# Re-dealing the filter rows of a Fourier layer in SBUF, and copying them by DMA, ahead of a long gated MLP

## The chip, the cores and the metric

The kernel runs on one core of a Trainium2 chip. A core has five engines that run side by side, each with its own queue of instructions: TensorE (PE, matrix products; its weight loads are shown as PEld), VectorE (DVE), ScalarE (ACT), GpSimd (POOL) and SyncE (SP), which here only issues transfers. Transfers run on 16 DMA engines that all queues share. Engines wait for each other through semaphores. SBUF, the on-chip memory, has 128 partitions; PSUM, into which TensorE writes, has eight banks.

The metric is the device time of one execution in microseconds. The kernel before took 485.1 us (median of three runs, 485.1 to 485.33).

## The reference

The input x has 2048 rows (positions) of 576 values. A layer normalisation is followed by a two-dimensional real Fourier transform, a product with a complex filter of 2048 x 289 values (w_r and w_i), and the inverse transform. The result is added to x. A second normalisation is followed by a gated MLP with 4608 hidden units, again added.

```python
h = x + _A_ref(_layernorm(x, axis=-1), A_w_r, A_w_i)
h2 = h + _B_ref(_layernorm(h, axis=-1), B_w_gate, B_w_up, B_w_down)
# _A_ref:  X = rfft2(x);  X = X * (w_r + 1j * w_i);  y = irfft2(X, s=(S, D))
# _B_ref:  (gelu(x @ w_gate) * (x @ w_up)) @ w_down
```

## The kernel before, in words

All transforms are matrix products with tables. The work falls into a start of some 55 us (normalisation, Fourier layer, first part of the second normalisation) and a long MLP part, which is almost pure TensorE work.

The start has these steps, in stages whose order on all engines is written out by hand in strings of codes (`SEQ1`, `SEQF`, `SEQ`). The first transform along positions (line 551) leaves its result in `U`. Then sixteen groups of frequencies, numbered by `GORD` as 1 to 15 and then 0, go through `SEQF`. For group number i: `D`/`d` is the transform along the 576 values (line 640), evicted to `CUS` (three buffers); `B` is a small transform over 16 (line 660), evicted to `YS` (five buffers); `T` (line 673, VectorE) multiplies `YS` by the filter in `WS`, in two instructions, one to `TP` and one to `TR`; `V`/`v` (line 681) and `R`/`r` (line 698) begin the inverse transform, evicted to `V` and `RB`. `RB` goes on to `VR` by small transfers. Evictions are casts at line 606 on ScalarE or VectorE, by the lists `DENG`, `BENG` and `VENG`. Four pairs of PSUM banks are shared by D, B, V and R. The order of the T products is 2, 0, 1, 3, 5, 4, 6, 7, 8 and so on. Then `SEQ` runs the rest of the inverse transform (lines 835 and 852), the addition to x (line 858), the second normalisation and the turn of its result, and the MLP begins (line 944).

The filter tile `WS` has 128 partitions x 2 sides x 2 planes (real 0, imaginary 1) x 16 groups x 289 values. Side jp (0 or 1) is loaded only into one half of the partitions: 64 jp to 64 jp + 63. The product needs each side in both halves, so that half is copied to the other half of the partitions by `dup_w`, in four steps: k = 0 for groups 1 to 5, k = 1 for 6 to 8, k = 2 for 9 to 12, k = 3 for 13 to 15 and 0.

The loads of the filter come in pieces, issued in order. A first half (`hf` 0) has groups 0 to 8, a second half groups 9 to 15. For each plane of each half there are two "up" pieces (`w_up`, one for each side: 32 rows, each contiguous in HBM over its groups) and four "down" pieces (`w_down`, `sl` 0 to 3, two for each side: 16 partitions x 8 or 7 separate rows of 578 bytes, the groups in reverse). `w_zero` fills group 0 of the down rows. In a half of 64 partitions the up pieces fill the lower 32 partitions and the down pieces the upper 32, every second one each. Plane 1 comes before plane 0. All are issued by SP behind the loads of x and the first tables, except the last two down pieces of plane 0 of the second half, which GpSimd issues.

The copies of step 0 are made by engines: GpSimd copies plane 1 and VectorE plane 0, each for both sides. Those of steps 1 to 3 are transfers within SBUF issued by GpSimd, which wait on the semaphores of the pieces. On GpSimd's queue the order is: the normalisation's work, the two down pieces, its two copies, the transfers of step 1, small operations (`NM`), the transfers of steps 2 and 3, the VR transfers. SP waits for the last of the copies before it loads the tables for the rest of the inverse transform (`tab_load`).

`Prog` keeps, for every name that is read or written, who wrote it last. An instruction waits for those it depends on. A key such as `("Wd", 0, jp, pl, 1)` stands for one copied part; the list `dup` says which copied parts the products of each step wait for.

The two lines that decide what a product waits for, and how a copy by an engine looks:

```python
r=[("Y", sl), *dup[(i >= 5) + (i >= 8) + (i >= 12)]] + (wkeys[0] if 1 <= g < 9 else ...)
P.op(DVE, lambda v: v.tensor_copy(dst, src), r=r, w=[(*n, g0)])
```

Of the kernel before, what the change touches and what calls it, by code (L numbers as in the profile page):

```python
# [7 lines left out]
ALU = mybir.AluOpType  # L8

S, D, K2 = 2048, 576, 289  # L10
# [5 lines left out]
NT = 16  # L16
# [30 lines left out]
def build_tables():  # L47
# [52 lines left out]
    for st in range(2):  # L100
        g = 1 - st
        for p in range(128):
            half, r, jj = p // 64, (p % 64) // 4, p % 4
            low = (g + 16 * jj) if half == 0 else _minus_rows(g)[jj]
            k = 128 * r + low
            w = np.exp(-2j * np.pi * ((k * nn) % 2048) / 2048.0)
            if low in (0, 64):
                sl, ri = 0, (0 if low == 0 else 1)
# [8 lines left out]
            if half == 0:  # L117
                sl = jj
                e = np.exp(-2j * np.pi * ((r * nn) % 16) / 16.0)
                ca, cb = e, 1j * e  # L120
            else:
                sl = (128 - low - g) // 16
# [17 lines left out]
    for st in range(2):  # L140
        for jp in range(2):
            for q in range(64):
                half, r, sl = q // 32, (q % 32) // 2, 2 * jp + q % 2
                jj = sl if half == 0 else (4 - sl) % 4 if st else 3 - sl
                po, cut = 64 * half + 4 * r + jj, slice(2 * jp, 2 * jp + 2)
                for m in range(2):
                    for ri in range(2):
                        BN[jp, :, :, st, m, ri, q] = B[st, m + ri, :, cut, :, po].reshape(16, 4)
                for ri in range(2):
                    VN[st, jp, ri, q, 0] = V[st, ri, po, :, :, cut].reshape(2, 16, 4)  # L150
                    VN[st, jp, ri, q, 1] = (1 - 2 * ri) * V[st, 1 - ri, po, :, :, cut].reshape(2, 16, 4)
# [7 lines left out]
    a = np.full((K2 - 1, 1), 2.0)  # L159
# [172 lines left out]
def _build(nc, A_x, A_w_r, A_w_i, B_w_gate, B_w_up, B_w_down, out):  # L332
    P = Prog(nc)
    T = build_tables()
    dram = {n: nc.inline_tensor(_np_bf16(T[n]), name="c_" + n.lower()) for n in T}
    PE, DVE, ACT, SP, POOL = "pe", "dve", "act", "sp", "pool"
# [12 lines left out]
    WS = sb.alloc("WS", [128, 2, 2, NG, K2], BF16)  # L349
# [54 lines left out]
    ATS = sb.alloc("ATS", [128, NT, 128], BF16)  # L404
# [41 lines left out]
    P.dma(SP, FT[:, :, :].rearrange("p a b -> p (a b)"), dram["FTAB"][:, :], "ft", w=["FT"])  # L446
    P.dma(SP, BT[:, :, :, :].rearrange("p a b c -> p (a b c)"), dram["BTAB"][:, :], "bt", w=["BT", "BT1"])

    def w_up(pl, hf):
        g0, g1 = ((0, 9), (9, 16))[hf]  # L450
        src = (A_w_r, A_w_i)[pl].tensor
        for jp in range(2):
            P.dma(SP, WS[64 * jp:64 * jp + 32, jp, pl, g0:g1, :].rearrange("p g k -> p (g k)"),
                  bass.AP(src, (32 * jp + g0) * K2, [[128 * K2, 16], [16 * K2, 2], [1, (g1 - g0) * K2]]), f"w{pl}{hf}", w=[("W", hf, pl, jp)])

    def w_down(pl, hf, sls=(0, 1, 2, 3), eng=SP, sem=""):
        g0, g1 = ((1, 9), (9, 16))[hf]
        src = (A_w_r, A_w_i)[pl].tensor
        for sl in sls:
            p0 = 64 * (sl // 2) + 32  # L460
            P.dma(eng, WS[p0 + sl % 2:p0 + 32:2, sl // 2, pl, g0:g1, :], bass.AP(src, (64 + 16 * (3 - sl) + 16 - g0) * K2, [[128 * K2, 16], [-K2, g1 - g0], [1, K2]]),
                  f"w{pl}{hf}{sem}", w=[("W", hf, pl, 2 + sl)])

    def w_zero(pl):
        for jp in range(2):
            P.dma(SP, WS[64 * jp + 32:64 * jp + 64, jp, pl, 0, :], bass.AP((A_w_r, A_w_i)[pl].tensor, (64 + 32 * jp) * K2, [[128 * K2, 16], [(-16 if jp else 48) * K2, 2], [1, K2]]),
                  f"wz{pl}", w=[("W", 2, pl, jp)])

    for pl in (1, 0):
        w_up(pl, 0)  # L470
        w_down(pl, 0)
    P.dma(SP, VT[:, 0:2, :, :].rearrange("p a b c -> p (a b c)"), dram["VTAB"][:, 0:512], "vt", w=["VT", "VT1"])
    for pl in (1, 0):
        w_up(pl, 1)
        w_down(pl, 1, (0, 1, 2, 3) if pl else (0, 1))
    for pl in (1, 0):
        w_zero(pl)
    GORD = list(range(1, NG)) + [0]
    wkeys = [[("W", hf, pl, h) for pl in range(2) for h in range(6 if hf < 2 else 2)] for hf in range(3)]
# [101 lines left out]
    for w in SEQ1:  # L581
        a = w[1:]
# [9 lines left out]
    for t, w in enumerate(SEQF):  # L592
        k, i = w[0], w[1:].rstrip("abc")
        if k in "DBVR":
            b = min((b for b in used if b not in busy), key=lambda b: used[b])
# [4 lines left out]
        elif k in "dvr":  # L600
            b = FB[k.upper(), int(i)]
# [16 lines left out]
                op = mm(h, o, seqs[h][j], not second and j == 0, second and j == len(seqs[0]) - 1, [prev[o]] if second and j == 0 else [])  # L618
                turn_over.setdefault(key, [None, None])[o] = op

    dup = [[("Wd", 0, jp, pl, 1) for jp in range(2) for pl in range(2)]] + [[("Wd", k, jp, 0, g) for jp in range(2) for g in ((6,), (9,), (13, 0))[k - 1]] for k in range(1, 4)]

    wdv = B_w_down[:, :].rearrange("(c p) d -> p c d", p=128)

# [91 lines left out]
                src = PS[32 * j:32 * j + 32, b0 * 512:(b0 + 2) * 512].rearrange("p (a c) -> p a c", a=2)[:, :, 128 * (i == LAST) + 64 * t_:128 * (i == LAST) + 64 * t_ + 64]  # L716
                ev((ACT, DVE, DVE, ACT)[j], dst, src, keys, [("V", g, 2 + t_)])

    def dup_w(k, jp, pl=slice(0, 2), eng=None):
        a, b = 64 * jp, 64 - 64 * jp  # L720
        n = ("Wd", k, jp, pl.start)
        for g0, g1 in (((1, 6),), ((6, 9),), ((9, 13),), ((13, 16), (0, 1)))[k]:
            dst, src = (WS[q:q + 64, jp, pl, g0:g1, :].rearrange("p a g k -> p a (g k)")[:, :, 1:] for q in (b, a))
            r = [x for x in (wkeys[1] if g0 > 8 else wkeys[0] if g0 else wkeys[0] + wkeys[2]) if pl.start <= x[2] < pl.stop]
            if eng is None:
                op = P.dma(POOL, dst, src, f"wd{k}{jp}", r=r, w=[(*n, g0)])
            elif eng == DVE:
                P.op(DVE, lambda v: v.tensor_copy(dst, src), r=r, w=[(*n, g0)])
            else:
                P.op(POOL, lambda v: v.tensor_scalar(dst, src, 1.0, 1.0, op0=ALU.mult, op1=ALU.mult), r=r + [("ATS", NT - 1)], w=[(*n, g0)])  # L730
        return op if eng is None else None

    w_down(0, 1, (2, 3), POOL, "p")
    for jp in range(2):
        dup_w(0, jp, slice(1, 2), POOL)
        dup_w(0, jp, slice(0, 1), DVE)
    for jp in range(2):
        dup_w(1, jp)
    c = 0
    while c < NT:  # L740
        c1 = c + 1
        while c not in ACT_TILES and c1 < NT and c1 not in ACT_TILES:
            c1 += 1
        src, f, keys = (SA[:, 0, c:c1], -1.0 / D, "SA0") if c in ACT_TILES else (MV1[:, c:c1, 0], -1.0, "MV1")
        P.op(POOL, lambda g, c=c, c1=c1, src=src, f=f: g.tensor_scalar(NM[:, c:c1], src, f, 1.0, op0=ALU.mult, op1=ALU.mult),
             r=[(keys, k) for k in range(c, c1)], w=[("NM", k) for k in range(c, c1)])
        c = c1
    for k in (2, 3):
        for jp in range(2):
            last = dup_w(k, jp)  # L750
    def hold(eng=SP):
        P.op(eng, None, after=[P.ops[PE][-1]])

# [55 lines left out]
    SLOT, last, held, ing = {}, [sorted(used.values()).index(used[2 * b]) - 4 for b in range(4)], set(), False  # L809
    for t, w in enumerate(SEQ):  # L810
        k, i = w[0], int(w[1:].rstrip("ADSP"))
        if k in "INu":
            b = min((b for b in range(2 * ing, 4) if b not in held), key=lambda b: last[b])
# [3 lines left out]
        elif k in "ioUEae":  # L817
            b = SLOT[{"i": "I", "o": "N", "U": "u", "E": "I", "a": "N", "e": "u"}[k], i] // 2
# [145 lines left out]
    for w in SEQ:  # L964
        a = w[1:]
# [53 lines left out]
    for j, c in enumerate(range(NPRE, NT)):  # L1019
        f = DEF0 + DSTEP * j  # L1020
# [77 lines left out]
def bass_sequential_preLN__spectral_gfnet__geglu_ffn__prompt_kernel(  # L1098
    nc, A_x, A_w_r, A_w_i, B_x, B_w_gate, B_w_up, B_w_down, out
):  # L1100
    _build(nc, A_x, A_w_r, A_w_i, B_w_gate, B_w_up, B_w_down, out)
# [28 lines left out]
```

## Time and profile before

| what | us |
|---|---|
| median of three runs | 485.1 |
| the profiled execution's own time | 486.04 |
| its span, from the first to the last instruction | 484.2 |
| TensorE busy | 477.1 |
| VectorE busy | 182.8 |
| ScalarE busy | 145.4 |
| GpSimd busy | 53.2 |

The profile is of one execution. A line of a timeline has the start, the length, the engine, the line of the kernel, the operation and its tiles, and in brackets how long the engine was idle before and what ended it. A "q" behind an engine's name is its queue issuing a transfer. `WS<-in_A_w_r_dram` is a load of the real plane of the filter, `WS<-in_A_w_i_dram` of the imaginary one, `WS<-WS` a copy between the halves. A wait for several semaphores is put down to the one that came last by the profile; where the engine named had long been done, it was another, often a transfer. TensorE's granted clock was 1.000 throughout.

### The profile page before, as it was taken

The page shows a single profiled execution, that of the slowest core. Times are in us where ns is not written, and L with a number is a line of the kernel's source. Part 1 is how long each engine was busy: PE and PEld are TensorE (multiplying, and loading weights), DVE is VectorE, ACT ScalarE, POOL GpSimd, SP SyncE. Part 2 cuts the span into 40 slices and gives each one's busy share as a digit, 9 for nine tenths or more (in the row PEclk, how much of TensorE's full clock was granted, in tenths as well). Part 3 has the DMA queues.
Part 4 walks back from the last instruction along what each step waited for, and adds up shares of the span by engine and source line. Part 5 has one row for each costly group of instructions (what it writes and reads, how often), then busy time and mean ns, then how long its engine had stood idle before and what let it go on. Part 6 is the DMA issues. An engine that isn't in the chain of part 4 may idle for free.

```text
span 484.2 us, 12888 instructions
## 1 busy us (share of the span) xinstructions
PE 477.1 (99%) x5874; PEld 279.1 (58%) x5874; DVE 182.8 (38%) x365; ACT 145.4 (30%) x291; POOL 53.2 (11%) x88
## 2 busy tenths in 40 slices
PE   7999999999999999999999999999999999999998
PEld 4877765544577644444677544444777444444774
DVE  7988755665500144333200234333101233333011
ACT  6998753434300032233200133223100133223000
POOL 7862317010120000000000000000000000000000
PEclk9999999999999999999999999999999999999999
DMA  8955789931430001000000011000000000000000
GB/s 289 217 134 161 249 283 346 333 87 24 161 111 27 26 15 23 20 1 0 3 14 15 26 24 22 14 0 2 3 14 26 14 1 0 1 1 1 3 26 26
DMA packets 28438, 33.19 MB, mean 69 GB/s; under 512 B 12624, under 2 KB 21472, under 8 KB 28384
## 3 DMA queue, kind: packets, MB, share of 16 engines
q1 hardware_dynamic: 24720, 19.87, 14.5%
q0 software_dynamic: 3664, 12.50, 8.0%
q8 instruction: 46, 0.75, 0.7%
q14 instruction: 8, 0.07, 0.1%
HBM read 26.21 MB, written 2.36 MB: 59 GB/s over the span
## 4 chain that ended last, share of the span: by engine, by line
PE 91%; SPq 3%; DMA 2%; DVE 2%; ACT 1%; issue 0%; DVEq 0%
PE PS L944 58%; PE PS L1044 27%; SPq L242 3%; PE PS L1056 2%; DMA WS<-in_A_w_r_dram 1%; PE PS L640 1%; DMA VR<-RB 1%; PE PS L994 1%; DVE XO L858 1%; PE PS L681 1%; ACT YS L606 1%; PE PS L835 0%; PE PS L660 0%; PE PS L1011 0%; PE PS L852 0%
## 5 line engine op out<-in xcount | busy, mean ns | idle before, releaser
L944 PE MATMUL PS<-HT,WG 64*128 64x512 bf16 (+1 forms) x2142 | 233.3, 372 | 0.1
L944 PEld LDWEIGHTS PS<-HT,WG 64*128 64x128 bf16 x2142 | 105.8, 94 | 114.5 <-DVE AT L953 0.2
L952 ACT ACTIVATE GL<-PS 128x512 bf16<-128x512 f32 x144 | 85.7, 596 | 281.7 <-PE PS L944 281.7
L953 DVE TENSOR_TENSOR AT<-GL,PS 128x512 bf16<-128x512 bf16 x144 | 98.8, 687 | 166.0 <-ACT GL L952 166.0
L1044 PE MATMUL PS<-WD,AT 64*128 64x288 bf16 x2160 | 132.9, 283 | 0.0
L1044 PEld LDWEIGHTS PS<-WD,AT 64*128 64x128 bf16 x2160 | 102.5, 94 | 30.6
L1031 DVE TENSOR_TENSOR OS<-PS,XO 128x288 bf16<-128x288 f32 (+2 forms) x32 | 13.3, 453 | 125.5 <-PE PS L1044 118.0
L944 PE MATMUL PS<-HT,WGX 64*128 64x512 bf16 x486 | 53.4, 376 | 0.0
L944 PEld LDWEIGHTS PS<-HT,WGX 64*128 64x128 bf16 x486 | 23.0, 94 | 29.4
L861 ACT ACTIVATE OS<-XO,NM 128x576 bf16<-128x576 bf16 x15 | 11.6, 774 | 11.4 <-DVE XO L1015 11.4
L640 PE MATMUL PS<-FT,U 64*128 64x288 bf16 x160 | 13.7, 284 | 0.3 <-DVE V L606 0.2
L673 DVE TENSOR_TENSOR TP<-YS,WS 128x1024 bf16<-128x1024 bf16 x16 | 11.0, 688 | 1.0 <-PE PS L698 1.0
L494 DVE BATCH_NORM_STATS2 ST<-XO 128x6 f32<-128x288 bf16 x26 | 10.1, 442 | 1.9 <-DMA XO<-in_A_x_dram 1.8
L681 PE MATMUL PS<-VT,TP 64*128 64x128 bf16 x256 | 10.0, 217 | 0.0
L242 POOL DMA_DIRECT2D WG<-in_B_w_gate_dram x9 | 6.1, 679 | 32.2 <-DMA WG<-in_B_w_gate_dram 28.9
L562 ACT ACTIVATE U<-PS 128x384 bf16<-128x384 f32 (+2 forms) x27 | 9.4, 479 | 0.7 <-PE PS L551 0.7
L242 POOL DMA_DIRECT2D WD<-in_B_w_down_dram x9 | 6.7, 755 | 26.1 <-PE PS L1011 26.1
L551 PE MATMUL PS<-ATS,XO 128*128 128x128 bf16 x96 | 8.3, 219 | 1.4 <-POOL ATS L520 1.4
L606 ACT ACTIVATE CUS<-PS 128x576 bf16<-128x576 f32 x14 | 9.0, 654 | 0.7 <-PE PS L640 0.5
L606 ACT ACTIVATE YS<-PS 128x576 bf16<-128x576 f32 x14 | 8.9, 653 | 0.6 <-PE PS L660 0.4
L1056 PE MATMUL PS<-WD,AT 128*128 128x448 bf16 (+1 forms) x72 | 9.0, 286 | 0.0
L681 PEld LDWEIGHTS PS<-VT,TP 64*128 64x128 bf16 x256 | 8.0, 94 | 1.3
(89 smaller groups left out, 230.0 us busy)
## 6 DMA issues: line engine op xcount, KB each, us to landing
WD<-in_B_w_down_dram POOLq DMA_DIRECT2D x9, 576.0 KB, 10.7
WG<-in_B_w_up_dram SPq DMA_DIRECT2D x6, 576.0 KB, 6.4
WG<-in_B_w_gate_dram POOLq DMA_DIRECT2D x6, 576.0 KB, 5.7
out_dram<-OS SPq DMA_DIRECT2D x30, 72.0 KB, 1.7
XO<-in_A_x_dram SPq DMA_DIRECT2D x6, 288.0 KB, 4.5
WGX<-in_B_w_up_dram SPq DMA_DIRECT2D x2, 576.0 KB, 4.7
WGX<-in_B_w_gate_dram POOLq DMA_DIRECT2D x2, 576.0 KB, 5.8
HT<-HN SPq DMA_TRANSPOSE x60, 2.4
```

Source lines behind the costliest of these rows:

```text
L242: fn = lambda e: e.dma_start(out_ap, in_ap)
L606: fn = (lambda v: v.tensor_copy(dst, src)) if eng == DVE else (lambda a: a.activation(dst, src, ACTF.Copy))
L640: return P.op(PE, lambda t: t.matmul(bank(b0 + o, 0, 128, 0, 2 * HK), U[64 * h:64 * h + 64, us, 2 * i:2 * i + 2, :, :], FT[64 * h:64 * h + ...
L673: P.op(DVE, lambda v, dst=dst, y4=y4, w4=w4: v.tensor_tensor(dst, y4, w4, op=ALU.mult), r=[("Y", sl), *dup[(i >= 5) + (i >= 8) + (i >= 12) ...
L681: return P.op(PE, lambda t: t.matmul(bank(b0 + o, 0, 128, 128 * c, 128 * c + 128), TP[64 * h:64 * h + 64, z, o, t_, c:256:2], VT[64 * h:64 ...
L861: P.op(ACT, lambda a, c=c, out=out: a.activation(out, XO[:, c, 0:D], ACTF.Square, bias=NM[:, c:c + 1], accum_out=SB2[:, 1, c:c + 1]), r=[( ...
L944: op = P.op(PE, lambda t, h0=h0, kt=kt, wt=wt, b=b, s=(not second and j == 0), e=(second and j == n - 1): t.matmul(bank(b, 0, 128, c0, c1) ...
L952: P.op(ACT, lambda a: a.activation(GL[:, s2, :], bank(b0), ACTF.Gelu_apprx_tanh), r=[("PS", b0)], w=[("GL", s2)])
L953: P.op(DVE, lambda v: v.tensor_tensor(AT[:, f, :], GL[:, s2, :], bank(b0 + 1), op=ALU.mult), r=[("GL", s2), ("PS", b0 + 1)], w=[("AT", f)])
L1031: P.op(DVE, lambda v: v.tensor_tensor(OS[:, p % 2, d0:d1], bank(b, 0, 128, 0, d1 - d0), XO[:, c, d0:d1], op=ALU.add), r=[("PS", b), ("X", ...
L1044: e[h] = P.op(PE, lambda t, f=f, h=h, r0=r0, j=j: t.matmul(bank(b0 + h, 0, 128, 0, 288), AT[r0:r0 + 64, f, 128 * p:128 * p + 128], WD[r0:r ...
L1056: P.op(PE, lambda t, b=b, d0=d0, d1=d1, f=f, j=j: t.matmul(bank(b, 0, 128, 0, d1 - d0), AT[:, f, 128 * p:128 * p + 128], WD[:, f, d0:d1], ...
```

## The change

The rows of the filter are put into other partitions. Within each half of 64 partitions the up rows now take the even partitions and the down rows the odd ones: an up piece fills every second partition of all 64, a down piece every fourth. The tables that depend on the order of the partitions are built to match. Down pieces are issued in the order 0, 2, 1, 3, so that the pieces of each plane alternate between the two halves of the partitions. GpSimd's two down pieces go to SP's queue as well, in their place in the order. The copies of step 0, which GpSimd and VectorE made, become two transfers issued by GpSimd, each with both planes of one side, on the same queue and ahead of those of step 1. The products' waits follow (`dup`). In the last step the transfers are issued in the order groups 13 to 15 of both sides, then group 0 of both sides.

```diff
@@ build_tables
-                half, r, sl = q // 32, (q % 32) // 2, 2 * jp + q % 2
+                half, r, sl = q % 2, q // 4, 2 * jp + q // 2 % 2
@@ loads
-    def w_up(pl, hf):
+    def w_up(pl, hf, jp, r0=0, r1=16):
...
-        for jp in range(2):
-            P.dma(SP, WS[64 * jp:64 * jp + 32, jp, pl, g0:g1, :]...,
-                  bass.AP(src, (32 * jp + g0) * K2, [[128 * K2, 16], [16 * K2, 2], [1, (g1 - g0) * K2]]), ...)
+        P.dma(SP, WS[64 * jp + 4 * r0:64 * jp + 4 * r1:2, jp, pl, g0:g1, :]...,
+              bass.AP(src, (128 * r0 + 32 * jp + g0) * K2, [[128 * K2, r1 - r0], [16 * K2, 2], [1, (g1 - g0) * K2]]), ...)
-    def w_down(pl, hf, sls=(0, 1, 2, 3), eng=SP, sem=""):
+    def w_down(pl, hf, sl):
...
-            p0 = 64 * (sl // 2) + 32
-            P.dma(eng, WS[p0 + sl % 2:p0 + 32:2, sl // 2, pl, g0:g1, :], ...)
+        jp, p0 = sl // 2, 64 * (sl // 2) + 2 * (sl % 2) + 1
+        P.dma(SP, WS[p0:64 * jp + 64:4, jp, pl, g0:g1, :], ...)
...
-            P.dma(SP, WS[64 * jp + 32:64 * jp + 64, jp, pl, 0, :], ...)
+            P.dma(SP, WS[64 * jp + 1:64 * jp + 64:2, jp, pl, 0, :], ...)
...
+    def w_half(pl, hf):
+        w_up(pl, hf, 0)
+        w_up(pl, hf, 1)
+        for sl in (0, 2, 1, 3):
+            w_down(pl, hf, sl)
+    w_half(1, 0)
+    w_half(0, 0)
     P.dma(SP, VT[...], dram["VTAB"][:, 0:512], "vt", w=["VT", "VT1"])
-    for pl in (1, 0):
-        w_up(pl, 1)
-        w_down(pl, 1, (0, 1, 2, 3) if pl else (0, 1))
+    w_half(1, 1)
+    w_half(0, 1)
@@ copies
-    def dup_w(k, jp, pl=slice(0, 2), eng=None):
+    def dup_w(k):
         for g0, g1 in (((1, 6),), ((6, 9),), ((9, 13),), ((13, 16), (0, 1)))[k]:
...
-            if eng is None:
-                op = P.dma(POOL, dst, src, f"wd{k}{jp}", r=r, w=[(*n, g0)])
-            elif eng == DVE:
-                P.op(DVE, lambda v: v.tensor_copy(dst, src), r=r, w=[(*n, g0)])
-            else:
-                P.op(POOL, lambda v: v.tensor_scalar(dst, src, 1.0, 1.0, ...), ...)
+            for jp in range(2):
+                a, b = 64 * jp, 64 - 64 * jp
+                dst, src = (WS[q:q + 64, jp, :, g0:g1, :]... for q in (b, a))
+                op = P.dma(POOL, dst, src, f"wd{k}", r=..., w=[("Wd", k, jp, g0)])
-    w_down(0, 1, (2, 3), POOL, "p")
-    for jp in range(2):
-        dup_w(0, jp, slice(1, 2), POOL)
-        dup_w(0, jp, slice(0, 1), DVE)
-    for jp in range(2):
-        dup_w(1, jp)
+    dup_w(0)
+    dup_w(1)
...
-    for k in (2, 3):
-        for jp in range(2):
-            last = dup_w(k, jp)
+    dup_w(2)
+    last = dup_w(3)
```

More of the change, by code (lines that the diff above doesn't have):

```diff
@@ L447, in _build @@
     P.dma(SP, BT[:, :, :, :].rearrange("p a b c -> p (a b c)"), dram["BTAB"][:, :], "bt", w=["BT", "BT1"])
-    def w_up(pl, hf):
+    def w_up(pl, hf, jp, r0=0, r1=16):
         g0, g1 = ((0, 9), (9, 16))[hf]
         src = (A_w_r, A_w_i)[pl].tensor
-        for jp in range(2):
-            P.dma(SP, WS[64 * jp:64 * jp + 32, jp, pl, g0:g1, :].rearrange("p g k -> p (g k)"),
-                  bass.AP(src, (32 * jp + g0) * K2, [[128 * K2, 16], [16 * K2, 2], [1, (g1 - g0) * K2]]), f"w{pl}{hf}", w=[("W", hf, pl, jp)])
@@ L456, in w_down @@
-    def w_down(pl, hf, sls=(0, 1, 2, 3), eng=SP, sem=""):
+        P.dma(SP, WS[64 * jp + 4 * r0:64 * jp + 4 * r1:2, jp, pl, g0:g1, :].rearrange("p g k -> p (g k)"),
+              bass.AP(src, (128 * r0 + 32 * jp + g0) * K2, [[128 * K2, r1 - r0], [16 * K2, 2], [1, (g1 - g0) * K2]]), f"w{pl}{hf}" + "b" * (r0 > 0), w=[("W", hf, pl, 6 if r0 else jp)])
+    def w_down(pl, hf, sl):
         g0, g1 = ((1, 9), (9, 16))[hf]
         src = (A_w_r, A_w_i)[pl].tensor
-        for sl in sls:
-            p0 = 64 * (sl // 2) + 32
-            P.dma(eng, WS[p0 + sl % 2:p0 + 32:2, sl // 2, pl, g0:g1, :], bass.AP(src, (64 + 16 * (3 - sl) + 16 - g0) * K2, [[128 * K2, 16], [-K2, g1 - g0], [1, K2]]),
-                  f"w{pl}{hf}{sem}", w=[("W", hf, pl, 2 + sl)])
+        jp, p0 = sl // 2, 64 * (sl // 2) + 2 * (sl % 2) + 1
+        P.dma(SP, WS[p0:64 * jp + 64:4, jp, pl, g0:g1, :], bass.AP(src, (64 + 16 * (3 - sl) + 16 - g0) * K2, [[128 * K2, 16], [-K2, g1 - g0], [1, K2]]),
+              f"w{pl}{hf}", w=[("W", hf, pl, 2 + sl)])
@@ L464, in w_zero @@
     def w_zero(pl):
         for jp in range(2):
-            P.dma(SP, WS[64 * jp + 32:64 * jp + 64, jp, pl, 0, :], bass.AP((A_w_r, A_w_i)[pl].tensor, (64 + 32 * jp) * K2, [[128 * K2, 16], [(-16 if jp else 48) * K2, 2], [1, K2]]),
+            P.dma(SP, WS[64 * jp + 1:64 * jp + 64:2, jp, pl, 0, :], bass.AP((A_w_r, A_w_i)[pl].tensor, (64 + 32 * jp) * K2, [[128 * K2, 16], [(-16 if jp else 48) * K2, 2], [1, K2]]),
                   f"wz{pl}", w=[("W", 2, pl, jp)])
-    for pl in (1, 0):
-        w_up(pl, 0)
-        w_down(pl, 0)
+    def w_half(pl, hf):
[3 more added lines that the diff above has]
+            w_down(pl, hf, sl)
@@ L472, in _build @@
+    w_half(1, 0)
+    w_half(0, 0)
     P.dma(SP, VT[:, 0:2, :, :].rearrange("p a b c -> p (a b c)"), dram["VTAB"][:, 0:512], "vt", w=["VT", "VT1"])
-    for pl in (1, 0):
-        w_up(pl, 1)
-        w_down(pl, 1, (0, 1, 2, 3) if pl else (0, 1))
+    w_half(1, 1)
+    w_half(0, 1)
     for pl in (1, 0):
@@ L619, in halves @@
                 turn_over.setdefault(key, [None, None])[o] = op
-    dup = [[("Wd", 0, jp, pl, 1) for jp in range(2) for pl in range(2)]] + [[("Wd", k, jp, 0, g) for jp in range(2) for g in ((6,), (9,), (13, 0))[k - 1]] for k in range(1, 4)]
+    dup = [[("Wd", k, jp, g) for g in ((1,), (6,), (9,), (13, 0))[k] for jp in range(2)] for k in range(4)]
     wdv = B_w_down[:, :].rearrange("(c p) d -> p c d", p=128)
@@ L717, in st_R @@
                 ev((ACT, DVE, DVE, ACT)[j], dst, src, keys, [("V", g, 2 + t_)])
-    def dup_w(k, jp, pl=slice(0, 2), eng=None):
-        a, b = 64 * jp, 64 - 64 * jp
-        n = ("Wd", k, jp, pl.start)
+    def dup_w(k):
         for g0, g1 in (((1, 6),), ((6, 9),), ((9, 13),), ((13, 16), (0, 1)))[k]:
-            dst, src = (WS[q:q + 64, jp, pl, g0:g1, :].rearrange("p a g k -> p a (g k)")[:, :, 1:] for q in (b, a))
-            r = [x for x in (wkeys[1] if g0 > 8 else wkeys[0] if g0 else wkeys[0] + wkeys[2]) if pl.start <= x[2] < pl.stop]
-            if eng is None:
-                op = P.dma(POOL, dst, src, f"wd{k}{jp}", r=r, w=[(*n, g0)])
-            elif eng == DVE:
-                P.op(DVE, lambda v: v.tensor_copy(dst, src), r=r, w=[(*n, g0)])
-            else:
-                P.op(POOL, lambda v: v.tensor_scalar(dst, src, 1.0, 1.0, op0=ALU.mult, op1=ALU.mult), r=r + [("ATS", NT - 1)], w=[(*n, g0)])
-        return op if eng is None else None
-    w_down(0, 1, (2, 3), POOL, "p")
-    for jp in range(2):
-        dup_w(0, jp, slice(1, 2), POOL)
-        dup_w(0, jp, slice(0, 1), DVE)
-    for jp in range(2):
-        dup_w(1, jp)
+            for jp in range(2):
+                a, b = 64 * jp, 64 - 64 * jp
+                dst, src = (WS[q:q + 64, jp, :, g0:g1, :].rearrange("p a g k -> p a (g k)")[:, :, 1:] for q in (b, a))
+                op = P.dma(POOL, dst, src, f"wd{k}", r=wkeys[1] if g0 > 8 else wkeys[0] if g0 else wkeys[0] + wkeys[2], w=[("Wd", k, jp, g0)])
+        return op
+    dup_w(0)
+    dup_w(1)
     c = 0
```

## The prediction

> **What bounds the kernel now.** I began with the slices of the page. TensorE is 99% busy over the span; only the first slices differ, so a change of the first 45 us can act only by moving the moment at which the long TensorE part begins.
>
> ```profile
> span 484.2 us, 12888 instructions
> PE 477.1 (99%) x5874; PEld 279.1 (58%) x5874; DVE 182.8 (38%) x365; ACT 145.4 (30%) x291; POOL 53.2 (11%) x88
> ...
> PE   7999999999999999999999999999999999999998
> ...
> DMA  8955789931430001000000011000000000000000
> ```
>
> The reader is to see that the DMA engines are full in the first quarter and nearly idle later. Next the chain of waits in order of time, from 13.77 us. Its first column is the start, the second the length.
>
> ```profile
> 13.77 6.59 DMA WS<-in_A_w_r_dram
> 20.36 0.02 issue
> 20.38 0.53 DVE WS L728
> 20.91 0.01 issue
> 20.92 0.54 DVE WS L728
> ...
> 21.50 0.63 DVE CUS L606
> ```
>
> The path runs through the last filter piece of the first half of the groups (issued by SP at 13.77, landed at 20.36), then through the two VectorE copies that the change removes. After that the stage is shared: the timeline of VectorE shows it continuously busy from here, with the product of the filter (line 673) first at 22.15.
>
> ```profile
> 20.38 1.07 DVE L728 COPY WS<-WS 64x1444 bf16<-64x1444 bf16 x2 [1.05 <-DMA WS<-in_A_w_r_dram]
> 21.37 0.75 DVE L606 CAST CUS<-PS 128x576 bf16<-128x576 f32 x1
> 22.15 0.69 DVE L673 TENSOR_TENSOR TP<-YS,WS 128x1024 bf16<-128x1024 bf16 x1
> ...
> 27.51 0.70 DVE L673 TENSOR_TENSOR TP<-YS,WS 128x1024 bf16<-128x1024 bf16 x1 [0.95 <-PE PS L698]
> ```
>
> And the timeline of GpSimd, which has the other two copies and issues the transfers:
>
> ```profile
> 16.03 1.34 POOL L242 DMA_DIRECT2D WS<-in_A_w_r_dram  x2
> 17.44 2.86 POOL L730 TENSOR_SCALAR WS<-WS 64x1444 bf16<-64x1444 bf16 x2
> 20.64 1.54 POOL L242 DMA_DIRECT2D WS<-WS  x2 [0.34 <-DMA WS<-in_A_w_r_dram]
> ...
> 27.89 3.59 POOL L242 DMA_DIRECT2D WS<-WS  x6 [2.55 <-DMA WS<-in_A_w_r_dram]
> ```
>
> Last, stages of this start (columns: window, its length, five engines, clock, DMA share, GB/s):
>
> ```profile
> 5.00:12.00 7.00, 5.63 (x58) 3.50 (x56) 6.95 (x30) 5.66 (x21) 5.50 (x11) 1.00 0.97 365
> 14.00:18.00 4.00, 4.00 (x72) 3.79 (x70) 4.00 (x18) 4.00 (x13) 3.67 (x6) 1.00 1.12 222
> 22.00:25.00 3.00, 2.88 (x48) 1.93 (x46) 2.97 (x8) 2.69 (x6) 2.51 (x7) 1.00 1.03 221
> 29.00:31.00 2.00, 2.00 (x43) 1.71 (x42) 2.00 (x7) 1.61 (x4) 2.00 (x5) 1.00 0.88 202
> 31.00:33.00 2.00, 2.00 (x58) 1.69 (x54) 1.75 (x5) 1.92 (x5) 2.00 (x5) 1.00 0.99 279
> ```
>
> The 128-partition loads move 365 GB/s. The filter pieces, each inside one half of the partitions, move 222 at a DMA share no lower. The copies from half to half, alone, move 202. So the filter traffic is limited by how fast it moves, not by how early it is issued.
>
> **The change, part by part.** All is worked out against the profiled execution: span 484.2, time 486.04, that is 1.84 around it; the median shown is 485.1, so 0.94 less. A shift of the start adds to both alike.
>
> Part 1, the copies of groups 1 to 5. Removed: two VectorE copies of 0.53 (1.07 together, on the path) and two GpSimd operations of 1.39 (2.86, before the landing at 20.36 and so beside it). Added: two transfers issued by GpSimd, each 64 x 2 x 1444 x 2 B = 0.370 MB, 0.739 MB together. Every product of the filter in groups 1 to 5 waits for both. They can be issued only when all twelve pieces of the first half have landed, both planes, whereas before the imaginary plane was copied from 17.44 while the real one was still coming.
>
> When do the pieces land? SP's queue up to the last of them is unchanged in number and size. GpSimd's two pieces (0.13 MB, of which 0.11 MB moved in 12.5 to 20.4) no longer compete in that window; at its 211 GB/s 0.11 MB is 0.5 us, so 19.85 instead of 20.36. GpSimd woke 0.28 after the landing before (20.36 to 20.64), so the first issue is at 20.13; it is otherwise idle from 16.08 on.
>
> How long do the copies take? The nearest rows are the other copies. The pair issued at 20.64, amid filter loads, landed after 5.5 and 5.8 us, the second at 27.43: 6.79 us for 0.443 MB. The pair issued at 27.89, when the loads had drained, ended at 33.06: 5.17 us for 0.591 MB, the DMA engines starting 1.17 after the issue. Scaled by bytes beyond a start of 1.2, the new pair takes 1.2 + 5.59 x 0.739 / 0.443 = 10.5 by the first row, 1.2 + 3.97 x 0.739 / 0.591 = 6.2 by the second: ends of 26.3 and 30.6. Between them stands GpSimd's queue in 22 to 25, with loads beside it: 0.40 MB in 3 us, 133 GB/s, by which 1.2 + 0.739 / 0.133 = 6.8, and 0.3 for the wake. I take this, since it has the same competitor (SP's second-half pieces) and no tail of another transfer in it. The first product then starts at 20.13 + 6.8 + 0.3 = 27.2 instead of 22.15, 5.1 later.
>
> How much is absorbed? In the order written out, VectorE stands at this product, and the cast of the second B result is behind it. ScalarE's next B cast needs a YS buffer that the second product frees, so TensorE can run on only to about where it was at 25.3, until the four pairs of banks are taken. That is enough for VectorE to find its inputs ready afterwards. From 22.15 to 44.43 VectorE was idle for 0.95 (before 27.51, where the second copies landed at 27.43; the page's name for it had long been done) and 0.22 (before 31.36) in whole waits. Those two go, since the inputs are now early: -1.2. The rest of the 22.28 us is work and cannot shrink. Sum: +5.1 - 1.2 = +3.9.
>
> [...]
>
> Part 2, the dealing. Up pieces go to every second partition of 64 instead of 32 neighbours, down pieces to every fourth of 64 instead of every second of 32; numbers and sizes of the rows stay, and the product and the tables' rows are only renamed. What it does to the rate no row shows. The nearest row for the new pattern is the copies' (they write 64 neighbouring partitions) with 202 GB/s, against 222 for the old one: no gain. The other end is 365. I take no change.
>
> [...]
>
> Part 3, the down pieces in the order 0, 2, 1, 3, so that transfers alternate between halves. Up pieces alternate already, in the 222 row, so I take nothing. The end of the bound is the row with 279, where copies of both directions were in flight.
>
> Part 4, the two pieces moved to SP. They add two issues of 0.6 to SP's queue, so that its last one ends at 27.2 instead of 25.89. Behind stand only the zero rows and, from 29.04, three VR transfers: free. The second half's landing, 27.60 before, is not earlier, since 0.739 MB goes ahead; the copies for groups 9 to 15 and 0 start behind the others on GpSimd's queue. Their bytes (0.591 and 0.591 MB at 202 GB/s, behind the second pair) give about 33.5 and 37. The products that need them (34.38 and 37.67 before) are 3.9 later too, so this costs nothing; the tables that SP loads after the last copy (36.12 before) are 1 to 2 later, and their first reader at 43.36 is 3.9 later. If the product came as early as before, this cover would be gone and the copies of groups 9 to 12 would set its pace.
>
> At the end of the stage TensorE waited 0.65 for VR until 45.16. The transfers are issued relative to casts that shift alike; I count nothing. From 55.54 on TensorE has no gap, so the shift reaches the end: 485.1 + 3.9 = 489.0 (span 488.1, profiled 489.9).
>
> **The rivals.**
> A, the loads gain from alternation, though not to the full: 279 GB/s. The 1.54 MB of SP's queue from 12.5 on takes 5.5, landing 18.0; copies at 133 x 279/221 = 168 GB/s take 1.2 + 4.4; product at 18.0 + 0.3 + 5.6 + 0.3 = 24.2: +2.0 - 1.2, so 485.9 (with less of a gain up to 488.0). For it: the 279 row mixes halves. Against: up pieces mixed them too.
>
> B, it ends faster: half-wise traffic reaches the 128-partition rate. At 365 GB/s landing is at 16.7, after the last issue (14.37); the copies at 279 take 1.2 + 2.6, since SP's second-half pieces then come only as fast as SP issues them; 16.7 + 0.3 + 3.8 + 0.3 = 21.1. The CUS cast, freed of the two copies, ends at 21.5, so the product starts there: -0.65 - 1.2, 483.3. It decides from a product before 23.3 on. For it: an alternation at 4.6 KB for each DMA engine is finer than the old. Against: 222 and 202 alike in two layouts.
>
> C, the copies are starved as in the first row above (30.6): +8.4 - 1.2, up to 492.3; with half of that tail, 490.9 to 491.5. For it: SP's queue holds 0.5 MB at 21. Against: GpSimd's queue got 59% of the DMA time there.
>
> D, the wait is hidden: TensorE or ScalarE bound the stage (21.60 and 20.55 us busy of 22.28) and the product's delay falls in slack. 485.1. Against: the chain of waits passes the removed copies, and four bank pairs hold little.
>
> **How the numbers follow.** Forecast (product at 26.3 to 28.8: 488.0 to 490.6) 0.55; A 0.18; B 0.09; C 0.13; D 0.05. Likeliest 489.0. The range leaves out B, D and the upper half of C: 485.6 to 491.2. A run tells 0.2% (1 us) from no change. Faster is B with 0.09; same is D and the lower part of A (up to 486.1), 0.05 + 0.05; slower the rest, 0.81.
>
> **What would show it.** In the changed kernel the chain should go from a filter piece to a copy transfer WS<-WS and from there to line 673's product (675 there), with VectorE idle 5 to 6 us ahead of it, and no idle time before the sixth product. GpSimd's first copy should be issued at 20.1, the two landing near 27. The windows 14 to 18 and 22 to 25 should again show about 220 GB/s. Wrong would be: 270 or more there (A, B), or a first product before 23.3. If the product is late but the long part begins as before, D was right.

## The result, and the profile after

The changed kernel took 491.51 us (median of four runs, 490.7 to 492.74), the kernel before 485.1 beside it (484.55 to 485.33): by the means 1.0136 times as long, 95% interval 1.0113 to 1.0159. The forecast was 489.0, with a range up to 491.2. The direction and the path through the transfers came as forecast; the size was 2.5 us short, 0.3 outside the range.

| profiled execution, us | before | after |
|---|---|---|
| its own time / span | 486.04 / 484.2 | 491.35 / 489.6 |
| first half of the filter landed | 20.36 | 19.07 |
| copies of step 0 landed | by engines | 23.76 and 27.35 |
| first product of the filter | 22.15 | 27.37 |
| "sixth" product | 27.51 | 33.22 |
| end of the last product, to `TP` | 41.58 | 47.48 |
| first product of the MLP | 55.54 | 60.85 |

What the prediction and the expectations call the sixth product is T5, the first product that needs the copies of step 1. In order of time it is the fifth. The name is kept here.

The page of the changed kernel, the same lines as were shown of before, and the granted clock:

```profile
span 489.6 us, 12886 instructions
...
PE 478.3 (98%) x5874; PEld 292.4 (60%) x5874; DVE 182.0 (37%) x363; ACT 145.6 (30%) x291; POOL 49.1 (10%) x86
...
PE   7969999999999999999999999999999999999998
...
PEclk9989999999999999999999999999999999999999
DMA  8974788961260001100000001000000000000000
```

The reader is to see a gap in the third slice of TensorE and, in the same slice, a clock below full speed, which no slice of before shows. The chain of waits (start, length) now passes the transfers instead of VectorE's copies:

```profile
13.48 5.59 DMA WS<-in_A_w_r_dram
19.07 0.30 issue
19.37 0.82 POOL WS L242
...
20.20 7.14 DMA WS<-WS
...
27.37 0.69 DVE TP L675
...
28.20 0.68 DVE YS L608
...
28.93 0.66 PE PS L642 x4
```

From the landing to the first product there are 8.3 us, where before had 1.8. VectorE's timeline shows how long it stood, and that it went on waiting after the transfers were done:

```profile
27.37 0.69 DVE L675 TENSOR_TENSOR TP<-YS,WS 128x1024 bf16<-128x1024 bf16 x1 [5.79 <-DMA WS<-WS]
...
30.83 0.76 DVE L608 CAST CUS<-PS 128x576 bf16<-128x576 f32 x1 [0.48 <-PE PS L642]
...
33.22 0.70 DVE L675 TENSOR_TENSOR TP<-YS,WS 128x1024 bf16<-128x1024 bf16 x1 [0.89 <-PE PS L683]
```

TensorE's timeline has the standstill that follows from it, with its length in the bracket:

```profile
23.14 0.53 PE L642 MATMUL PS<-FT,U 64*128 64x288 bf16 x6
...
28.93 0.66 PE L642 MATMUL PS<-FT,U 64*128 64x288 bf16 x4 [5.25 <-DVE YS L608]
```

And by stages (window, length, five engines, clock, DMA share, GB/s):

```profile
14.00:18.00 4.00, 4.00 (x72) 3.78 (x69) 3.97 (x17) 4.00 (x13) 1.72 (x3) 1.00 1.12 261
22.00:25.42 3.42, 1.67 (x28) 0.85 (x23) 0.00 (x0) 1.48 (x3) 1.41 (x8) 1.00 0.99 207
25.42:28.83 3.41, 0.00 (x0) 0.00 (x0) 1.46 (x4) 0.60 (x2) 0.00 (x0) 1.00 0.95 192
28.83:32.24 3.41, 3.31 (x28) 2.02 (x30) 2.93 (x8) 1.64 (x4) 1.56 (x3) 0.50 0.15 33
```

The loads run at 261 GB/s instead of 222. TensorE does nothing from 25.42 to 28.83, and exactly when it is wanted again its clock is halved, for 3.41 us. In the kernel before the clock was full (1.00) in this whole stage.

### The profile page after: what moved, and what is told of

It reads as the page before. It is cut to its first block, busy times and chain, and to the rows that moved or that the text cites. A ratio compares the mean times of both kernels' runs of the same rounds, so it can differ in the third digit from the quotient of the medians.

```text
span 489.6 us, 12886 instructions
## 1 busy us (share of the span) xinstructions
PE 478.3 (98%) x5874; PEld 292.4 (60%) x5874; DVE 182.0 (37%) x363; ACT 145.6 (30%) x291; POOL 49.1 (10%) x86
## 4 chain that ended last, share of the span: by engine, by line
PE 92%; DMA 3%; SPq 2%; DVE 1%; issue 0%; POOL 0%; DVEq 0%
PE PS L936 57%; PE PS L1036 27%; SPq L242 2%; PE PS L1048 2%; PE PS L642 2%; PE PS L683 2%; DMA WS<-WS 1%; DMA WS<-in_A_w_r_dram 1%; PE PS L662 1%; PE PS L827 1%; PE PS L986 1%; DVE XO L850 1%; PE PS L1003 0%; PE PS L844 0%; DVE OS L910 0%
## 5 line engine op out<-in xcount | busy, mean ns | idle before, releaser
L936 PEld LDWEIGHTS PS<-HT,WG 64*128 64x128 bf16 x2142 | 109.7, 94 | 110.4 <-DVE AT L945 0.2
L1036 PEld LDWEIGHTS PS<-WD,AT 64*128 64x128 bf16 x2160 | 109.6, 94 | 23.4
L936 PEld LDWEIGHTS PS<-HT,WGX 64*128 64x128 bf16 x486 | 24.7, 94 | 27.8
L642 PEld LDWEIGHTS PS<-FT,U 64*128 64x128 bf16 x160 | 7.3, 99 | 8.1 <-DVE YS L608 5.6
```

The costliest lines, as they stand in the source:

```text
L642: return P.op(PE, lambda t: t.matmul(bank(b0 + o, 0, 128, 0, 2 * HK), U[64 * h:64 * h + 64, us, 2 * i:2 * i + 2, :, :], FT[64 * h:64 * h + ...
L936: op = P.op(PE, lambda t, h0=h0, kt=kt, wt=wt, b=b, s=(not second and j == 0), e=(second and j == n - 1): t.matmul(bank(b, 0, 128, c0, c1) ...
L1036: e[h] = P.op(PE, lambda t, f=f, h=h, r0=r0, j=j: t.matmul(bank(b0 + h, 0, 128, 0, 288), AT[r0:r0 + 64, f, 128 * p:128 * p + 128], WD[r0:r ...
```

## The experiments

**The kernel before, profiled twice more.** The forecast had subtracted from the one profile of before, whose own time lay 0.94 above the median.

> The kernel before, unchanged, for a second profile of it. Disputed is whether the wait of 0.95 ahead of its sixth product, which the forecast took away as part of the change's gain, belongs to the kernel or to that one profiled execution, whose own time (486.04) lay 0.94 above the median. Theory (it belongs to the execution): a time of 484.6 to 485.5, the first half landed at 19.3 to 20.4, the first product at 21.8 to 22.2, the sixth 4.5 to 4.8 after the first (5.36 in the profile shown), and the MLP's first product at 54.4 to 54.9 in place of 55.54. Rival (it belongs to the kernel, where GpSimd's two pieces hold up the copies of step 1): again 5.2 to 5.5 between first and sixth product, and the MLP's first product at 55.3 to 55.8.

> The kernel before once more, for a third profile, on the same terms: by the theory the sixth product 4.5 to 4.8 after the first and the MLP's first product at 54.4 to 54.9; by the rival 5.2 to 5.5 and 55.3 to 55.8.

They took 485.14 and 485.44. VectorE's timeline of the second profile:

```profile
22.11 0.69 DVE L673 TENSOR_TENSOR TP<-YS,WS 128x1024 bf16<-128x1024 bf16 x1
...
27.06 0.70 DVE L673 TENSOR_TENSOR TP<-YS,WS 128x1024 bf16<-128x1024 bf16 x1 [0.54 <-DMA WS<-WS]
```

From the first to the sixth product 4.95 and 4.87 us (5.36 in the profile shown), between the two expectations: the wait ahead of the sixth product belongs to the kernel, but 0.5 us long, not 0.95. From the first product to the MLP 32.53 and 32.31 (33.39); the part of this difference that lies behind the sixth product is the wait for VR, 0.20 or absent and not 0.65. The MLP began at 54.64 and 54.97, and against the second profile the changed kernel's adds up: 60.85 - 54.64 = 6.21, and 491.35 - 485.14 = 6.21.

**Step 0 by the engines again, everything else as changed.**

```diff
...
-    dup_w(0)
+    copy0(1)    # GpSimd tensor_scalar, one for each side, plane 1
+    copy0(0)    # VectorE tensor_copy, one for each side, plane 0
```

> The changed kernel with step 0 copied by the engines again (plane 1 by GpSimd, plane 0 by VectorE); the new dealing, the alternating order and SyncE's whole list stay. If the two transfers of step 0 are the whole loss: first half of the filter landed at 19.1 as in the changed kernel, VectorE's copies 19.2 to 20.3, first product at 21.5 (after the cast that TensorE releases at 20.8), step 1 issued at 19.4 and landed by 26.5, granted clock 1.0 from 5 us on; 483.3 to 484.8 us. If the dealing or the longer SyncE queue costs something too (the second half lands later): 486 or more, with a wait before the product of group 9.

Measured 485.48 beside 485.7: ratio 1.0001, 0.9986 to 1.0015. The time is above the 483.3 to 484.8 expected, but level with the kernel before. The whole loss is in the transfers of step 0; the new dealing, the order and SP's longer queue cost and bring nothing in the time. The loads were fast here too (264 GB/s, landed at 19.41), but the first product came only 0.3 earlier than in the profile shown (21.83). The timelines say why:

```profile
17.09 2.86 POOL L735 TENSOR_SCALAR WS<-WS 64x1444 bf16<-64x1444 bf16 x2 [1.07 <-DVE ATS L527]
```

```profile
19.43 1.62 DVE L737 COPY WS<-WS 64x1444 bf16<-64x1444 bf16 x2 [0.18 <-DMA WS<-in_A_w_r_dram]
```

GpSimd copies until 19.95, and VectorE's copies, begun before that, take 1.62 instead of 1.07. An earlier landing of the second plane runs into the copies of the first. The three runs below that copy with engines show the same (1.77, 1.72 and 1.72). In all four profiles the first of VectorE's two copies began 0.52 to 0.67 before the end of GpSimd's last one, and ended 0.39 after it, whenever it had begun: its end went with GpSimd's.

**Only step 0 as transfers, all else as before.**

```diff
...
-        dup_w(0, jp, slice(1, 2), POOL)
-        dup_w(0, jp, slice(0, 1), DVE)
+        dup_w(0, jp)    # a transfer with both planes
```

> The kernel before with one part changed: step 0 copied by two transfers on GpSimd's queue. Old dealing, old order, GpSimd's two pieces stay. If the new dealing makes the loads land earlier: first half landed at 20.4, transfers take 7.5 to 8.5 us, first product at 28.2 to 29.2, halved clock behind it; 492 to 493.5 us, slower than the changed kernel. If the new dealing is what costs: near 489.

492.26, ratio 1.0135 (1.0105 to 1.0166): this part alone makes the whole difference. Landing at 20.33, copies landed at 28.16, first product at 28.24, MLP at 61.85. TensorE stood 5.93 us, and two stretches of 3.41 had the halved clock, the first of them while it still stood:

```profile
26.56:33.39 6.83, 3.60 (x34) 2.26 (x36) 4.47 (x10) 2.50 (x5) 2.46 (x5) 0.50 0.59 114
```

**Only GpSimd's two pieces moved to SP.**

```diff
-        w_down(pl, 1, (0, 1, 2, 3) if pl else (0, 1))
+        w_down(pl, 1)
...
-    w_down(0, 1, (2, 3), POOL, "p")
```

> The kernel before with one part changed: the two pieces of GpSimd go to SyncE's queue. If they competed with the first half: it lands 0.5 us earlier (19.9), the first product at 21.7 instead of 22.15, second half landed at 28 to 29, which is still ahead of its product at 34: 484.4 to 485.1 us. If the gain of the changed kernel's loads (19.1) is from this alone: landing at 19.1. If the second half's delay is felt: 486.

485.59, ratio 1.0000 (0.9986 to 1.0014). The first half landed at 19.30, 1.0 earlier than in the kernel before (20.36, 20.32 and 20.86). The first product came at 21.88 and the MLP at 54.69, as in the other profiles of before (54.64 and 54.97): nothing of the 1.0 arrives.

**Which part makes the loads faster.** Two kernels complete a square with that one and the changed one. The first is the changed kernel with the down pieces in the old order, the second the last one with the new order.

```diff
-        for sl in (0, 2, 1, 3):
+        for sl in (0, 1, 2, 3):
```

> The changed kernel with the down pieces in the order 0, 1, 2, 3 in place of 0, 2, 1, 3: new dealing without alternation of the down pieces. Disputed is what makes the load of the first half faster once GpSimd's pieces are gone: windows 14 to 18 moved 261 and 227 GB/s in two looks at the changed kernel (in the second the load was done before 18; in 14 to 16 it had 253 and 278), 236 with the old dealing and the old order all on SP (255 in 14 to 16, 217 in 16 to 18, landing 19.3). Theory (alternation does it): 225 to 240 in 14 to 18, landing at 19.2 to 19.6. Rival (the dealing does it): 255 to 270 in 14 to 18, landing at 18.1 to 19.1. Either way the time stays within 1.5 of the changed kernel's 491.4, since the transfers of step 0 remain: 490.5 to 492.5.

```diff
-    def w_down(pl, hf, sls=(0, 1, 2, 3), eng=SP, sem=""):
+    def w_down(pl, hf, sls=(0, 2, 1, 3), eng=SP, sem=""):
```

> The kernel before (old dealing, step 0 copied by the engines) with GpSimd's two pieces on SP and the down pieces in the order 0, 2, 1, 3: alternation without the new dealing. Theory (alternation does it): 255 to 270 GB/s in 14 to 18, landing at 18.1 to 19.1. Rival (the dealing does it): 225 to 240 in 14 to 18, landing at 19.2 to 19.6, as with the old order (236, 19.3). Time as before either way, 484.9 to 486.2, because in the two runs with step 0 by the engines an earlier landing (18.1 to 19.4) gave nothing.

Windows 14 to 18, all pieces on SP. Old dealing in the old order, new dealing in the old order, old dealing alternating:

```profile
14.00:18.00 4.00, 4.00 (x71) 3.79 (x69) 3.97 (x17) 4.00 (x14) 2.69 (x4) 1.00 1.12 236
```

```profile
14.00:18.00 4.00, 4.00 (x73) 3.90 (x71) 4.00 (x18) 4.00 (x13) 2.55 (x4) 1.00 1.09 219
```

```profile
14.00:18.00 4.00, 4.00 (x74) 3.90 (x72) 4.00 (x18) 4.00 (x13) 2.86 (x4) 1.00 1.06 256
```

With both, 256 to 264 in four profiles (261 in the changed kernel's first). Three more, the changed kernel's second among them, show 227, 222 and 172; there the DMA engines' share of the window was only 0.73 to 0.92, so it doesn't show what they could move. So in these profiles the alternation adds 20 to 42 GB/s, and the dealing adds nothing by itself (219 is even below the 225 to 240 expected). Three of the four corners are one profile each, and a window is a coarse measure: the 236 is 255 in its first half and 217 in its second. The landings point the same way, less clearly: 19.30 and 19.47 in the old order, 18.62 with the alternation alone, 18.07 to 19.41 in the seven profiles with both. The times, 492.72 (0.2 above what was expected) and 485.21, one run each with 484.92 for the kernel before beside them, follow the copies alone.

**Dummy products in TensorE's standstill.** To the changed kernel 22 products of a tile of zeros are added ahead of step `D8`, the one at which it stands, into a bank pair that is free then.

```diff
+        if w == "D8":
+            warm(22)    # t.matmul(bank(...), ZD[:, 0:128], ZD[:, :], start=True, stop=True)
```

> The changed kernel with 22 dummy products of zeros (some 4.7 us) on TensorE in the place where it stands still, in a bank pair that is free there. Nothing else is changed. If the halved clock after the standstill costs time of its own: first product unchanged at 27.4, granted clock 1.0 at 29 to 32, VectorE's waits of 0.48, 0.89 and 0.27 us behind it mostly gone, 1.0 to 1.6 us less than the changed kernel (489.9 to 490.5). If VectorE sets the pace whatever the clock: no difference (491.5). If the dummies still run when the banks come free: slower.

The time was 490.71, ratio 1.0101 (1.0068 to 1.0135). The clock stayed full: this profile and that of the next run with dummies hold no record of the clock, but the four D products behind the standstill took 0.42 us in both, and 0.66 in the changed kernel at half clock. However, the dummies ran from 24.59 to 29.51, with the first product at 26.68; in the changed kernel TensorE resumes 1.56 behind that product. They held up what they should help. The next two runs share the runs of the kernel before (485.4): the changed kernel unaltered, and with 14 dummies.

> The changed kernel itself once more, as a second profile and as the yardstick for the other kernels of this set. All theories: first product at 27 to 28, granted clock halved from about 28 to 32, 490.5 to 492.5 us.

> The changed kernel with 14 dummy products (3.0 us) instead of 22 in the place where TensorE stands still, so that they are done before the banks come free (at about 28). If the halved clock costs time of its own: clock 1.0 at 28 to 32, TensorE's next product at 28 to 28.9, VectorE's waits of 0.48 and 0.89 us behind the first product gone; 1.0 to 1.8 us less than the changed kernel of this set. If the clock doesn't matter since VectorE sets the pace: within 0.5 us of it.

The changed kernel took 491.39 (1.0130, 1.0112 to 1.0148), with the dummies 490.03 (1.0095, 1.0077 to 1.0112): 1.4 us less by the medians, though the single runs overlap (490.19 to 493.02 and 489.17 to 491.69). The stage itself shows the difference on VectorE and TensorE:

```profile
27.89 0.69 DVE L675 TENSOR_TENSOR TP<-YS,WS 128x1024 bf16<-128x1024 bf16 x1 [5.95 <-DMA WS<-WS]
...
32.34 0.70 DVE L675 TENSOR_TENSOR TP<-YS,WS 128x1024 bf16<-128x1024 bf16 x1
```

```profile
23.96 3.19 PE L777 MATMUL PS<-ZD 128*128 128x512 bf16 x14
29.44 0.42 PE L642 MATMUL PS<-FT,U 64*128 64x288 bf16 x4 [2.29 <-DVE YS L608]
```

From the first to the sixth product 4.45 us, and no wait at the sixth; the changed kernel took 5.85 and, in its second profile, 5.92. Half a clock for 3.41 us costs 1.4 us there. Part of it was given back later in this profile (TensorE stood 0.59 for no visible reason, VectorE waited 0.92 for it), so that from the first product to the MLP only 0.7 is left of it (32.84 against 33.48 and 33.58). From the sixth product to the MLP it took 28.39, and 29.09 in the run with 22 dummies, against 27.63 and 27.66 in the changed kernel. Whether and how the dummies cause this stays open.

**The second half of the loads held back** until the copies of step 0 have landed, so that nothing of SP's competes with them.

```diff
-    w_half(1, 1)
-    w_half(0, 1)
...
-    dup_w(0)
+    P.op(SP, None, after=[dup_w(0)])
+    w_half(1, 1)
+    w_half(0, 1)
```

> The changed kernel, but SyncE waits for the landing of the step 0 copies before it issues the second half of the filter and the zero rows. If the copies are slow because they share the DMA engines with the second half: issued at 19.4, landed at 24.0 to 24.8 (1.2 us start, 0.739 MB at 202 GB/s), first product at 24.5 instead of 27.4. The second half then lands at 32 to 34, the copies of groups 9 to 12 at 37 to 39, and the product of group 9 waits for them (due at 36): 488 to 490.5 us. If the copies are slow by themselves: first product still at 27 and 493 us or more.

493.67, ratio 1.0179 (1.0155 to 1.0202). The time expected for the first theory failed, and its first product came at 25.14, not 24.5. Even with nothing of SP's beside them the copies took 6.75 us from the first issue (18.36) to the landing (25.11), against 7.98 and 7.60 in the changed kernel. By these profiles SP's loads cost the difference, 0.9 to 1.2. The first two lines are windows, the third is VectorE's:

```profile
20.00:25.00 5.00, 3.85 (x62) 2.45 (x58) 0.76 (x1) 3.64 (x6) 2.40 (x9) 1.00 0.90 212
23.00:30.00 7.00, 4.12 (x80) 2.81 (x78) 4.79 (x11) 4.17 (x8) 0.00 (x0) 1.00 0.54 147
```

```profile
41.19 0.69 DVE L671 TENSOR_TENSOR TP<-YS,WS 128x1024 bf16<-128x1024 bf16 x1 [4.46 <-DMA WS<-WS]
```

The DMA engines moved 212 GB/s, about what the copies alone moved in the kernel before (202). The queue also held the 0.443 MB of step 1, issued at 19.80 and 20.37, which landed at 25.31 and 26.72. But they took little from step 0. In the trace the two can be told apart by the size of their packets (5776 bytes in step 0, 5196 and 3464 in step 1): the first packet of step 1 moved at 22.90, when 115 of the 128 of step 0 had begun. In the changed kernel's two profiles 122 and 117 had. So the copies are slow for the most part by themselves: 1.40 us to the first packet, 4.97 for the packets (149 GB/s), 0.38 from there to the landing.

The price for holding back is the wait of 4.46 for groups 9 to 12. TensorE stood for 2.84 us around the first product, the clock stayed full there (1.00 in 23 to 30), and the sixth product came 4.45 after the first: the same number as with the dummies, without any.

**Engine copies, and five dummy products at the wait for VR,** since the first experiment's profiled execution showed the halved clock there (45.48 to 48.90).

```diff
+        if w == "i0":
+            ...    # five products of zeros into a free bank pair
```

> The kernel with the new dealing and engine copies (first of these experiments), with 5 dummy products of zeros (1.1 us) on TensorE where it waits for the last VR transfers at about 43.5. If the clock's halving at 45 to 49 in that kernel's profile comes from TensorE's wait of 1.6 us there: granted clock 1.0 from 5 us to the end, the long part begins at 54.5 to 55 rather than 57.1, and no execution is above 486; 483.8 to 485.0 us median. If the halving has another cause: as that kernel, 485.5.

486.07, ratio 1.0014 (1.0005 to 1.0023), all eleven runs within 485.92 to 486.44: even times, but no gain, and the expected 483.8 to 485.0 was missed. The clock was full at this place, by the length of the products (0.42 us for four, against 0.74 at half clock in the first experiment). VR landed at 44.31 and the MLP began at 55.93, and TensorE's timeline has the reason: the dummies ran on until 45.41, and the products that need VR stood behind them.

```profile
44.17 1.24 PE L972 MATMUL PS<-ZD 128*128 128x512 bf16 x5 [0.30 <-DVE VR L608]
45.34 0.42 PE L838 MATMUL PS<-DT,V 64*128 64x288 bf16 x4
45.59 0.29 PE L838 MATMUL PS<-DT,VR 64*128 64x288 bf16 x2
```

No version was faster than the kernel before beyond the noise.

## Why the prediction was right or wrong

*The landing* was put at 19.85. It was 19.07 in the profile after and 18.10 in the second. The pieces taken off GpSimd's queue were worth 1.0, not 0.5. *Part 3*, the alternation, which was counted at nothing because "up pieces alternate already", was worth 20 to 42 GB/s by the few profiles above. This was the mechanism of rival A, at 261 GB/s instead of its 279, but A's time did not follow, because the copies did not speed up with it (136 GB/s, where A had 168).

*Part 2*, the dealing, at no change: right. It stands 236 against 219 in the old order and 256 against 261 in the new.

*The copies* were put at 6.8 us from the row of 133 GB/s. They took 7.98, and 7.6 in the second profile. The rate was right: from the first packet to the end of the last, step 0 moved in 5.44 and 5.37 us, at 136 and 138 GB/s. The two ends were too small in the sum. The first packet moved 1.55 and 1.72 us after the issue, not 1.2, and from the last packet to the landing it took 0.99 and 0.51, for which the sum had nothing. The first issue itself took 0.82, against 0.93 for the one at 20.64 in the kernel before. Landing and copies erred in opposite directions, and the first product, forecast at 27.2, came at 27.37. This agreement is owed to luck.

*The absorption of 1.2* is the step that failed. Most of it, 0.95, was to be saved between the first and the sixth product; that stretch took 5.85 us, 0.49 more than in the profile of before that the sum used. First, half of it wasn't there: in the other two profiles of before the wait ahead of the sixth product was 0.54 and 0.46, and the wait for VR, which the forecast carried on unchanged, was 0.20 and nothing. Second, in its place stood a cost. "VectorE to find its inputs ready afterwards" supposed that TensorE would run on to 25.3 and resume at full speed. It stopped at 23.67, at a point that it had reached at about 24.07 in the kernel before, so it had less done ahead than supposed, and it came back with half its clock. From first to sixth product the changed kernel took 5.85 and 5.92 us, the kernel before 4.95 and 4.87 in its further profiles. The two versions whose clock stayed full, and whose TensorE was free in time, took 4.45 each; the two whose clock was halved for 6.83 us took 6.02 and 6.53. So full speed would have absorbed some 0.45, and the halved clock cost 1.4. From the sixth product to the MLP nothing changed: 27.63 and 27.66, against 27.58 and 27.44. With the first product 5.26 later than in the second profile of before (27.37 against 22.11), 5.26 + 0.90 + 0.05 is the 6.21 by which the MLP began later.

*The base*: the sum was made against a profile whose waits were longer than in a median run. It was moved to the median without asking which waits made the 0.94. Of the 0.90 by which it exceeds the second profile, 0.41 lies between first and sixth product, where the sum then subtracted, and 0.45 behind that, in the wait for VR. The 2.5 us come about like this: against the profile of before that the sum was made for, the MLP began 5.31 later (60.85 against 55.54) and not 3.9, and nearly all of these 1.4 lie between the first and the sixth product. The other 1.1 are the 0.94 of the base and the 0.16 by which the changed kernel's profile lay below its median.

*Part 4* cost nothing, as said, and the shift of the start reached the end in full, which rules out rival D. B is out with the first product at 27.37. Of the signs named, VectorE's idle time of 5 to 6 us ahead of the product (5.79) and the landing of the copies near 27 were there; no idle time before the sixth product (0.89) and 220 GB/s in 14 to 18 (261) were not. C gave the right time by a mechanism that wasn't there: the copies were not starved to 30.6.

## What to carry to other kernels

Before engine copies (here 1.07 us of VectorE on the path, 2.86 of GpSimd beside the load) are replaced by a transfer of the same bytes, its time from issue to landing must be priced: it waits for all pieces, where an engine could begin with the first plane, and its time has two ends besides the rate (here 1.4 to 1.7 us until the first packet moves, 0.4 to 1.0 from the last packet to the landing). A stall that is priced as a shift should also be priced at the clock that TensorE has when it returns (here half for 3.41 us, which cost 1.4 us). And before a wait is subtracted, look at a second profile, above all when the first one's own time lies above the median.

## What was unexpected of the hardware

The granted clock changed in steps of 3.41 us, and in these profiles what it became went with how busy TensorE had been in the 3.41 us before. Take the stretches backward and forward from each change, from 5 to 62 us in all profiles that record the clock, with TensorE's busy time: 0.00 (twice), 0.18, 0.47, 0.60, 0.71, 1.31 and 1.56 us were followed by half a clock. 1.67, 1.87, 2.11 and everything above were followed by the full one. (The stretches with 0.18 and 1.31 were themselves at half clock, and so were some of those above 3.1.) The 1.56 is from the first experiment, where the longest single standstill was, by chance, also 1.56 us:

```profile
42.07:45.48 3.41, 1.56 (x22) 1.25 (x24) 1.34 (x6) 1.11 (x6) 0.00 (x0) 1.00 0.37 94
```

```profile
45.08 0.34 PE L838 MATMUL PS<-DT,VR 64*128 64x288 bf16 x2 [1.56 <-DMA VR<-RB]
```

The half clock lasted 3.41 us (28.83 to 32.24 in the changed kernel) or 6.83 us (26.56 to 33.39 with only step 0 as transfers). TensorE need not have been idle before it: a stretch that was 46% busy (1.56 of 3.41) was followed by the half clock too. Why the steps have this length no run shows. Where the half clock sets in differs between executions (28.83 and 28.05 in the changed kernel's two profiles), and so does the price: in the eight timed runs of the changed kernel the mean clock over the span was 0.996 to 0.997 in five, which took 491.07 us on average, and 0.993 in three, which took 492.37.

Also unexpected: the order in which pieces alternate between the halves of the partitions counted (256 to 264 against 219 to 236 GB/s where the load filled the window), and where within the halves they lie did not (new against old: 219 against 236 in the old order, 261 against 256 alternating), as far as so few profiles show.
